# Attention and two expert layers on one core: seven buffers of queries, keys and values, loads six tiles ahead, and their blanks shared out anew

## The chip, the cores and the metric

The kernel runs on one core of a Trainium2 chip. The metric is the device time of one execution in microseconds; less is better. The core has five engines that work side by side: TensorE (PE) multiplies matrices, VectorE (DVE) and ScalarE (ACT) work on elements, GpSimd (POOL) does the same and issues transfers by index, and SyncE (SP) issues most of the ordinary transfers (DMA). Each engine runs its own instructions in program order and waits where data from another is missing.

## The reference

Three layers follow each other. Only the first bears on this change; the other two are expert layers over its result.

```python
q, k, v: (8, 8, 576, 64)              # batch, heads, sequence, head size; float32
scores = scale * matmul(q_c, k_c^T)   # inside chunks of 64 tokens
attn = exp(scores - max) / (sum + 1e-9)
x = matmul(attn, v_c)                 # as (4608, 512): one row for each token
# first expert layer: the best of 8 experts for each token, relu(x @ w1) @ w2, scaled by gates
# second expert layer: 8 experts that take 576 tokens each, in order of their scores
```

## The kernel before

The 4608 tokens are 36 tiles of 128. Attention is one loop over t = 0 to 35 in `attention`. For a tile, `load_qkv` asks SP for two transfers into one of `NQ` buffers named `qkv`, in turn (`t % NQ`): L392 fills the even partitions of columns 0 to 1543 and L393 the odd partitions of columns 1032 to 2575. What the two leave free must be zero, since the products of two heads are made together: `blanks` writes these zeros once for each buffer with two memsets, L379 for the right part (columns 1544 on, before the odd partitions are filled) and L380 for the left part (columns 0 to 1031).

In iteration t the parts stand in this order on every engine: the exponentials of tile t+1 (ACT), the transposes of tile t (`probs_T`, L424), the scores of tile t+2 (`scores`, L403 on PE, maximum L407 and its negative L410 on DVE), the product with the values of tile t-1 (`values`, L439 on PE; L441, L443 and L449 on DVE make and scale the row x), `gates` (L482), the next load (`load_qkv`), the store of x of tile t-1 (`x_out`, L452, also on SP), and the transposes and gate products of older tiles (L459, L470). The order is the program's: PE, DVE, ACT and SP are scheduled by hand.

The load in iteration t is that of tile t+4. With five buffers it overwrites the one of tile t-1, so SP holds it until `values(t - 1)`, a few instructions ahead in the same iteration, is done. The scores of that tile come in iteration t+2.

After every four tiles a routing step (`route`, L499 to L583 on DVE, some rows in each iteration) finds places for 512 tokens, and POOL scatters them into a list with four transfers by index (L585). From t = 23 on the weights of the first expert are fetched (L691), and POOL splits them in two parts (L359, L360). When the loop has ended, job 0 of the first expert layer starts on PE (L824, L844), and the memory of the buffers goes to its weights and its hidden layer.

Of the kernel before, what the change touches and what calls it, by code (L numbers as in the profile page):

```python
# [30 lines left out]
NT = N // 128  # L31
# [21 lines left out]
ROW = 514  # L53
VW = 65
QKV = 2 * 512 + 8 * VW
NQ = 5
T0, T1, T2 = 23, 24, 28
A0, A1, A2, A3 = 5, 2, 1, 1
J0, J1, J2, HOLD2 = 0.8, 0.8, 1, 16
# [9 lines left out]
class Kernel:  # L69
# [226 lines left out]
    def attention(self, st):  # L296
        nc = self.nc
        pool = st.enter_context(self.tc.tile_pool(name="qkvs", bufs=1))
        self.aw = st.enter_context(self.tc.tile_pool(name="aw", bufs=2))
        self.qkvb = []  # L300
        for i in range(NQ):
            a = pool.tile([128, QB], F32, name=f"qkv{i}")
            self.qkvb.append(a)
        for i in range(2):
            self.blanks(i, nc.vector)
            self.load_qkv(i)
        for i in range(2, NQ):
            self.blanks(i, nc.gpsimd)
            if i < 4:
                self.load_qkv(i)  # L310
        spare = self.wk.tile([128, 1], F32, name="spare", bufs=1)
        nc.vector.memset(spare, 0.0)
        nc.scalar.activation(spare, spare, AF.Exp)
        self.constants()
        opened, total, acc = self.opened0, self.total0, self.acc0
        self.state = (acc, opened, total)
        for a, v in ((self.tab, 0.0), (self.order, 0.0), (opened, 0.0), (total, 0.0), (acc, 0.0),
                     (self.L, 0.0), (self.blank, 0.0), (self.left, E * (E - 1) / 2), (self.C, 0.0), (self.first, 0.0), (self.m, -BIG), (self.f, -BIG), (self.dead, -BIG)):
            nc.gpsimd.memset(a, v)
        self.xp = {}  # L320
        self.ex, self.xT, self.x, self.S, self.pending = {}, {}, {}, {}, None
        self.routes, self.scat, self.hold = [], [], 0
        zero = self.qkvb[0][0:128:2, QKV:]
        nc.sync.dma_start(self.list.rearrange("(p r) c -> p (r c)", p=64), zero[:, 0:2 * NB * BT // 64])
        self.scores(0)
        self.scores(1)
        self.exps(0, range(8))
        for t in range(NT):
            if t + 1 < NT:
                self.exps(t + 1, range(4))  # L330
            self.probs_T(t)
            if t + 1 < NT:
                self.exps(t + 1, range(4, 8))
            if t + 2 < NT:
                self.scores(t + 2)
            if t:
                self.values(t - 1)
            self.gates()
            if t + 4 < NT:
                self.load_qkv(t + 4)  # L340
            if t:
                self.x_out(t - 1)
            if t >= 2:
                self.x_T(t - 2)
            if t >= 3:
                self.logits(t - 3)
            self.advance(A0)
            if t == 3:
                self.routes.append(self.select_constants(self.consts))
            if t == T0:  # L350
                self.open(0)
                self.x_list(0)
            c, odd = divmod(t - T0, 2)
            if 0 <= c < 4 and not odd:
                self.fetch(c, self.w1, self.reg)
            c, odd = divmod(t - T1, 2)
            if 0 <= c < 4 and not odd:
                hi, lo = self.chunks[c]
                nc.gpsimd.tensor_copy(hi, self.raw[c])  # L359
                nc.gpsimd.tensor_tensor(lo, self.raw[c], hi.bitcast(F32), op=OP.subtract)  # L360
            if t >= NT - 4:
                self.fetch(t - NT + 4, self.w2, self.reg)
            if t == NT - 1:
                self.x_list(1)
            if t == T2:
                self.x_load(0)
        self.gates()
        self.x_T(NT - 2)
        self.logits(NT - 3)
        for u in (0, 1):  # L370
            self.x_turn(0, u)
        for u in (0, 1):
            self.x_split(0, u)
        self.values(NT - 1)
        self.x_out(NT - 1)

    def blanks(self, i, eng):
        a = self.qkvb[i]
        eng.memset(a[:, QKV:], 0.0)  # L379
        eng.memset(a[:, 0:QKV - 512], 0.0)  # L380

    def finish(self, i):
        self.gates()
# [6 lines left out]
    def load_qkv(self, t):  # L390
        a = self.qkvb[t % NQ]
        self.nc.sync.dma_start(a[0:128:2, 0:QKV], self.qkv[t, 0])  # L392
        self.nc.sync.dma_start(a[1:128:2, QKV - 512:], self.qkv[t, 1])  # L393

    def scores(self, t):
        nc, wk = self.nc, self.aw
        a = self.qkvb[t % NQ]
        q = a[:, QKV - 512:QKV].rearrange("p (h n) -> p h n", h=4)
# [30 lines left out]
    def values(self, t):  # L429
        nc, wk = self.nc, self.aw  # L430
        eT = self.ex.pop(t)
        a = self.qkvb[t % NQ]
        O = [self.ps.tile([128, 4, VW], F32, name="O", bufs=2) for _ in range(2)]
# [989 lines left out]
```

## Time and profile before

| | |
|---|---|
| three runs | 1333.54, 1337.66 and 1338.27 us; median 1337.66 us |
| the profiled execution | 1333.46 us; span from first to last instruction 1331.6 us |
| PE busy in the span | 1157.2 us, 87% |
| attention, 0 to 210 us | PE busy 160.50, DVE 131.00, ACT 107.53, POOL 57.46 us |
| granted PE clock | 0.926 in the mean, 0.87 from 0 to 210 us |
| transfers from 0 to 210 us | 203 GB/s at a busy share of 0.73 |

A time at a row's start counts from the first instruction. The engine of a row that ends in q (SPq) is the queue that issues a transfer: the row's duration is that of the issue, not of the transfer. An arrow in brackets names what ended the idle time before the instruction. The granted clock is a share of 2.4 GHz: 1.00 is that level and 0.50 is 1.2 GHz.

### The profile page before, as it was taken

How to read it: one execution, taken by the hardware profiler on the slowest of the kernel's cores; microseconds unless marked ns; L12 is line 12 of the kernel's file. 1: busy time of each engine (PE TensorE's matmuls, PEld its weight loads, DVE VectorE, ACT ScalarE, POOL GpSimd, SP SyncE). 2: the span in 40 equal slices, each digit the busy share in tenths (PEclk: the TensorE clock that was granted, in tenths of full speed). 3: DMA queues.
4: the chain of work that ended last, by engine and by line, in shares of the span. 5: the costliest groups of instructions: out<-in, count | busy, mean ns of one | idle time of the engine just before them, and what ended most of it. 6: DMA issues, size and time to landing. Idle time of an engine off the chain costs nothing.

```text
span 1331.6 us, 23258 instructions
## 1 busy us (share of the span) xinstructions
PE 1157.2 (87%) x8424; PEld 998.5 (75%) x8424; DVE 776.3 (58%) x2214; ACT 489.6 (37%) x1052; POOL 192.7 (14%) x233
## 2 busy tenths in 40 slices
PE   6978789689898896769789963999999999999997
PEld 4766568688697796768689952878797878788895
DVE  4756687855254354345366667767787868654430
ACT  4655454334242243234244421323232323334430
POOL 3112243111101101110000101020202021112001
PEclk8978789899998897888899975899999999999999
DMA  6776867765353554564467652241515052434310
GB/s 207 235 180 203 202 204 152 198 204 143 109 163 105 151 168 107 161 193 112 123 181 226 206 152 91 76 143 60 168 35 194 14 190 73 138 96 148 114 48 36
DMA packets 90581, 190.06 MB, mean 143 GB/s; under 512 B 22992, under 2 KB 46608, under 8 KB 90384
## 3 DMA queue, kind: packets, MB, share of 16 engines
q1 hardware_dynamic: 77904, 153.96, 39.9%
q0 software_dynamic: 11136, 32.59, 7.7%
q8 instruction: 97, 1.59, 0.6%
q10 hardware_dynamic: 1344, 1.10, 0.3%
q14 instruction: 100, 0.82, 0.2%
HBM read 152.33 MB, written 35.28 MB: 141 GB/s over the span
## 4 chain that ended last, share of the span: by engine, by line
PE 57%; issue 14%; DVE 7%; DMA 5%; POOL 1%; ACT 1%; SPq 1%; ACTq 0%; another core or an unknown queue 0%; POOLq 0%; DVEq 0%
PE O L844 6%; PE ph L844 5%; PE ph L1289 4%; PE ph L1293 4%; PE ph L1291 4%; PE py L1326 3%; PE py L1324 3%; PE py L1328 3%; DMA wr<-in_w_dram 2%; PE O L867 2%; PE O L869 2%; PE O L868 2%; PE ph L867 2%; PE ph L869 2%; PE ph L868 2%
## 5 line engine op out<-in xcount | busy, mean ns | idle before, releaser
L698 DVE TENSOR_TENSOR wlo<-wr,whi 128x1024 fp32r<-128x1024 f32 x122 | 146.6, 1218 | 39.1 <-ACT whi L697 38.4
L1289 PE MATMUL ph<-xhi,whi 128*128 128x256 f32 (+1 forms) x512 | 155.6, 304 | 2.0 <-DVE hlo L1298 0.7
L697 ACT ACTIVATE whi<-wr 128x1024 fp32r<-128x1024 f32 x122 | 126.5, 1054 | 80.8 <-DMA wr<-in_w_dram 37.4
L1291 PE MATMUL ph<-xlo,whi 128*128 128x256 f32 (+1 forms) x512 | 154.7, 302 | 0.0
L1293 PE MATMUL ph<-xhi,wlo 128*128 128x256 f32 (+1 forms) x512 | 154.4, 302 | 0.0
L818 POOL DMA_INDIRECT xr<-xs,idx x48 | 46.3, 965 | 461.9 <-DVE idx L816 143.1
L844 PE MATMUL O<-xhi,whi 128*128 128x256 f32 (+4 forms) x240 | 79.8, 334 | 33.6 <-issue 33.6
L1326 PE MATMUL py<-wlo,hhi 128*128 128x512 f32 x256 | 105.2, 411 | 0.0
L1328 PE MATMUL py<-whi,hlo 128*128 128x512 f32 x256 | 103.0, 402 | 0.0
L1324 PE MATMUL py<-whi,hhi 128*128 128x512 f32 x256 | 102.7, 401 | 0.0
L1297 ACT ACTIVATE hhi<-ph 128x256 fp32r<-128x256 f32 x128 | 49.0, 384 | 145.3 <-PE ph L1293 140.6
L1289 PEld LDWEIGHTS ph<-xhi,whi 128*128 128x128 f32 x512 | 98.5, 192 | 3.9 <-issue 1.1
L1291 PEld LDWEIGHTS ph<-xlo,whi 128*128 128x128 f32 x512 | 98.7, 193 | 0.5 <-DVE xlo L1260 0.2
L1293 PEld LDWEIGHTS ph<-xhi,wlo 128*128 128x128 f32 x512 | 98.5, 192 | 0.4
L844 PE MATMUL ph<-xhi,whi 128*128 128x256 f32 (+4 forms) x240 | 76.8, 324 | 14.1 <-issue 11.4
L1245 DVE TENSOR_TENSOR wlo<-wr,whi 128x512 fp32r<-128x512 f32 x124 | 81.9, 684 | 8.1 <-ACT whi L1240 8.1
L1298 DVE SCALAR_TENSOR_TENSOR hlo<-ph,hhi 128x256 fp32r<-128x256 f32 x128 | 53.0, 419 | 51.5 <-ACT hhi L1297 33.3
L844 PEld LDWEIGHTS O<-xhi,whi 128*128 128x128 f32 x240 | 47.6, 198 | 45.6 <-issue 44.5
L844 PE MATMUL O<-xhi,wlo 128*128 128x256 f32 (+4 forms) x240 | 77.0, 323 | 0.0
L844 PE MATMUL ph<-xhi,wlo 128*128 128x256 f32 (+4 forms) x240 | 74.5, 314 | 0.0
L403 PE MATMUL ph<-qkv 128*64 128x128 f32 x576 | 47.4, 316 | 29.2 <-DMA qkv<-in_qkv_dram 28.5
L417 ACT ACTIVATE ex<-ph,nm 128x64 f32<-128x64 f32 x288 | 68.1, 346 | 11.7 <-DVE nm L410 10.1
(321 smaller groups left out, 2836.8 us busy)
## 6 DMA issues: line engine op xcount, KB each, us to landing
wr<-in_w_dram SPq DMA_DIRECT2D x128, 512.0 KB
qkv<-in_qkv_dram SPq DMA_DIRECT2D x72, 386.0 KB
wr<-in_w2b_dram SPq DMA_DIRECT2D x32, 512.0 KB
wr<-in_w1b_dram SPq DMA_DIRECT2D x30, 512.0 KB
x<-y SPq DMA_DIRECT2D x184, 64.0 KB
xs<-x SPq DMA_DIRECT2D x35, 256.0 KB
x<-blank SPq DMA_DIRECT2D x8, 514.0 KB
wr<-in_w1b_dram ACTq DMA_DIRECT2D x2, 512.0 KB
```

The costliest lines, as they stand in the source:

```text
L417: self.nc.scalar.activation(ex8[:, h // 2, h % 2, :], S8[:, h, :], AF.Exp, scale=0.125, bias=nm[:, h:h + 1])
L697: nc.scalar.activation(hi, self.raw[c], AF.Copy)
L698: (eng or nc.vector).tensor_tensor(lo, self.raw[c], hi.bitcast(F32), op=OP.subtract)
L844: nc.tensor.matmul(p[:, q, :], a[:, k, :], b[:, k, 0:w], start=c == 0, stop=c == 11)
L867: nc.tensor.matmul(q, whi[:, ds], self.hhi[:, f, 0:w], start=f == 0, stop=False)
L1245: self.nc.vector.tensor_tensor(lo[:, s], self.raw[c][:, s], hi[:, s].bitcast(F32), op=OP.subtract)
L1289: nc.tensor.matmul(p, whi[:, k, :], xhi[:, k, cs], start=k == 0, stop=False)
L1291: nc.tensor.matmul(p, whi[:, k, :], xlo[:, k, cs], start=False, stop=False)
L1293: nc.tensor.matmul(p, wlo[:, k, :], xhi[:, k, cs], start=False, stop=k == 3)
L1324: nc.tensor.matmul(p, hhi[:, f, ts], whi, start=f == 0, stop=False)
L1326: nc.tensor.matmul(p, hhi[:, f, ts], wlo, start=False, stop=False)
L1328: nc.tensor.matmul(p, hlo[:, f, ts], whi, start=False, stop=f == 7)
```

## The change

There are seven buffers instead of five. In iteration t the load is that of tile t+6 (`LOOK`), which overwrites the buffer of tile t-1, as before; its scores come in iteration t+4. Ahead of the loop six tiles are loaded instead of four. The zeros are written by other engines: for buffer 0 the left part by DVE and the right one by POOL, for buffer 1 the other way round, and for all others both by POOL; before, DVE wrote both parts of buffers 0 and 1. Buffers 4 to 6 come after the constants.

```diff
-NQ = 5
+NQ = 7
+LOOK = NQ - 1
...
-        for i in range(2):
-            self.blanks(i, nc.vector)
+        self.blanks(0, nc.vector, nc.gpsimd)
+        self.load_qkv(0)
+        self.blanks(1, nc.gpsimd, nc.vector)
+        self.load_qkv(1)
+        for i in (2, 3):
+            self.blanks(i, nc.gpsimd, nc.gpsimd)
             self.load_qkv(i)
-        for i in range(2, NQ):
-            self.blanks(i, nc.gpsimd)
-            if i < 4:
-                self.load_qkv(i)
...
         self.constants()
+        for i in range(4, NQ):
+            self.blanks(i, nc.gpsimd, nc.gpsimd)
+            if i < LOOK:
+                self.load_qkv(i)
...
-            if t + 4 < NT:
-                self.load_qkv(t + 4)
+            if t + LOOK < NT:
+                self.load_qkv(t + LOOK)
...
-    def blanks(self, i, eng):
+    def blanks(self, i, left, right):
         a = self.qkvb[i]
-        eng.memset(a[:, QKV:], 0.0)
-        eng.memset(a[:, 0:QKV - 512], 0.0)
+        right.memset(a[:, QKV:], 0.0)
+        left.memset(a[:, 0:QKV - 512], 0.0)
```

On SP, from the load of tile 3 on, before (the number behind `qkv` is that of the buffer, `list` takes zeros from buffer 0, `xs` takes x of tiles 0 and 1):

```order
L392 DMA qkv3_126<-in_qkv_dram 64x1544
L393 DMA qkv3_126<-in_qkv_dram 64x1544
L324 DMA list_63<-qkv0_123 64x200
L392 DMA qkv4_127<-in_qkv_dram 64x1544
L393 DMA qkv4_127<-in_qkv_dram 64x1544
L392 DMA qkv0_123<-in_qkv_dram 64x1544
L393 DMA qkv0_123<-in_qkv_dram 64x1544
L452 DMA xs_62<-x_308 128x512
L392 DMA qkv1_124<-in_qkv_dram 64x1544
L393 DMA qkv1_124<-in_qkv_dram 64x1544
L452 DMA xs_62<-x_357 128x512
```

And in the changed kernel, where the lines stand five further down:

```order
L397 DMA qkv3_126<-in_qkv_dram 64x1544
L398 DMA qkv3_126<-in_qkv_dram 64x1544
L397 DMA qkv4_127<-in_qkv_dram 64x1544
L398 DMA qkv4_127<-in_qkv_dram 64x1544
L397 DMA qkv5_128<-in_qkv_dram 64x1544
L398 DMA qkv5_128<-in_qkv_dram 64x1544
L329 DMA list_63<-qkv0_123 64x200
L397 DMA qkv6_129<-in_qkv_dram 64x1544
L398 DMA qkv6_129<-in_qkv_dram 64x1544
L397 DMA qkv0_123<-in_qkv_dram 64x1544
L398 DMA qkv0_123<-in_qkv_dram 64x1544
L457 DMA xs_62<-x_318 128x512
```

The store of tile 0's x stood behind the load of tile 5, and now stands behind that of tile 7; the load of tile 5 has moved ahead of the loop.

POOL's start, before (all its six memsets of blanks, then the identity for the transposes):

```order
L379 MEMSET qkv2_125 128x1032
L380 MEMSET qkv2_125 128x1032
L379 MEMSET qkv3_126 128x1032
L380 MEMSET qkv3_126 128x1032
L379 MEMSET qkv4_127 128x1032
L380 MEMSET qkv4_127 128x1032
masks.py:197 MEMSET ident_149 128x128
```

And in the changed kernel:

```order
L384 MEMSET qkv0_123 128x1032
L385 MEMSET qkv1_124 128x1032
L384 MEMSET qkv2_125 128x1032
L385 MEMSET qkv2_125 128x1032
L384 MEMSET qkv3_126 128x1032
L385 MEMSET qkv3_126 128x1032
masks.py:197 MEMSET ident_149 128x128
```

Six memsets still stand ahead of the identity, but the first two are one part each of buffers 0 and 1. The six of buffers 4 to 6 come after the constants, ahead of the zeros for the routing.

## Rows read from the trace of the kernel before

**Rows 1.** The page: engine busy time; the loads of attention.

```profile
PE 1157.2 (87%) x8424; PEld 998.5 (75%) x8424; DVE 776.3 (58%) x2214; ACT 489.6 (37%) x1052; POOL 192.7 (14%) x233
...
qkv<-in_qkv_dram SPq DMA_DIRECT2D x72, 386.0 KB
```

**Rows 2.** Windows: attention as one stretch (columns as in its heading).

```profile
core 0: us, PE busy (x) PEld busy (x) DVE busy (x) ACT busy (x) POOL busy (x), PEclk, DMA share, GB/s
...
0.00:210.00 210.00, 160.50 (x1823) 126.43 (x1824) 131.00 (x552) 107.53 (x386) 57.46 (x96) 0.87 0.73 203
```

**Rows 3.** Waits of PE, 0 to 205 us: total, times, longest.

```profile
PE ph L403 <- DMA qkv<-in_qkv_dram: 28.5, 12, 7.9
...
PE O L439 <- DVE x L449: 5.7, 5, 1.9
```

**Rows 4.** Timeline, first 11 us: start, duration, engine, line, [idle before].

```profile
0.75 0.96 POOL L379 MEMSET qkv<- 128x1032 f32 x1 [0.29 <-POOLq L1411]
...
2.12 0.92 DVE L380 MEMSET qkv<- 128x1032 f32 x1 [0.16 <-issue]
...
3.07 0.59 SPq L392 DMA_DIRECT2D qkv<-in_qkv_dram  x1
...
5.23 0.47 SPq L392 DMA_DIRECT2D qkv<-in_qkv_dram  x1
...
7.86 1.97 PE L403 MATMUL ph<-qkv 128*64 128x128 f32 x16 [7.86 <-DMA qkv<-in_qkv_dram]
...
10.77 1.55 PE L403 MATMUL ph<-qkv 128*64 128x128 f32 x12 [0.94 <-DMA qkv<-in_qkv_dram]
```

**Rows 5.** Timeline: the loads of tiles 5 and 7, and the scores of tile 5.

```profile
18.34 0.47 SPq L392 DMA_DIRECT2D qkv<-in_qkv_dram  x1
...
25.94 1.97 PE L403 MATMUL ph<-qkv 128*64 128x128 f32 x16 [4.12 <-DMA qkv<-in_qkv_dram]
...
29.68 0.47 SPq L392 DMA_DIRECT2D qkv<-in_qkv_dram  x1
```

**Rows 6.** Timeline: scores and values after a wait, and one tile later.

```profile
73.18 1.97 PE L403 MATMUL ph<-qkv 128*64 128x128 f32 x16 [1.88 <-DMA qkv<-in_qkv_dram]
...
74.91 1.98 PE L439 MATMUL O<-qkv,eT 128*64 128x130 f32 x16
...
79.21 1.09 PE L403 MATMUL ph<-qkv 128*64 128x128 f32 x16
...
80.14 1.06 PE L439 MATMUL O<-qkv,eT 128*64 128x130 f32 x16
```

**Rows 7.** Timeline of SP: first half-loads of some tiles.

```profile
20.84 0.47 SPq L392 DMA_DIRECT2D qkv<-in_qkv_dram  x1
...
54.14 0.47 SPq L392 DMA_DIRECT2D qkv<-in_qkv_dram  x1
...
58.03 0.47 SPq L392 DMA_DIRECT2D qkv<-in_qkv_dram  x1
...
64.87 0.47 SPq L392 DMA_DIRECT2D qkv<-in_qkv_dram  x1
...
157.90 0.48 SPq L392 DMA_DIRECT2D qkv<-in_qkv_dram  x1
...
165.63 0.48 SPq L392 DMA_DIRECT2D qkv<-in_qkv_dram  x1
```

**Rows 8.** Windows and timeline around one group's scatters of the list.

```profile
72.00:74.00 2.00, 0.82 (x8) 0.85 (x10) 0.20 (x1) 1.37 (x6) 0.00 (x0) 0.51 1.03 416
...
84.00:88.00 4.00, 2.42 (x32) 2.08 (x28) 0.69 (x1) 1.08 (x5) 1.86 (x2) 1.00 0.91 69
...
87.23 0.69 DVE L407 TENSOR_REDUCE mx<-ph 128x8 f32<-128x512 f32 x1 [4.10 <-remote]
```

**Rows 9.** Timeline: a weight split on POOL and the DVE beside it.

```profile
145.63 2.41 POOL L360 TENSOR_TENSOR wlo<-wr,whi 128x1024 fp32r<-128x1024 f32 x1
...
145.73 2.39 DVE L563 SCALAR_TENSOR_TENSOR ge<-jd,ge 128x72 f32<-128x72 f32 x1
```

## Prediction

> **What bounds it now.** The page says that PE is busy for 87% of the span [rows 1], so only a stretch in which PE stands still can give much. The window of attention shows one: of its first 210 us PE is busy for 160.50, at a granted clock of 0.87, while the DMA engines are busy for 0.73 of the time and move 203 GB/s [rows 2]. No engine is full there: DVE, the next, has 131.00 us. So I read the waits of PE up to 205 us. The scores wait for their loads 12 times, 28.5 us in total; the next group, the values behind DVE's x, has 5.7 us [rows 3]. Two of the twelve are the start, 7.86 and 0.94 us [rows 4]. Ten are left with 19.7 us: the first, 4.12 us ahead of tile 5's scores [rows 5], is the longest, and one of 1.88 us stands at 73.18 [rows 6].
>
> The timeline shows why a load is late. Tile 5's was issued at 18.34, and its scores began at 25.94 when it had landed, 7.6 us later [rows 5]. The load is held until the values of the tile before are done, and its scores come two iterations on. An iteration that neither waits for a load nor holds a scatter takes 3.93 us (mean of 11 distances between SP's loads; 54.14 to 58.03 is one [rows 7]). Two of them are 7.9 us, just what a load took. Whatever delays one stops PE.
>
> A wait costs more than its idle time. Behind the one at 73.18 the scores take 1.97 us and the values 1.98; one tile later 1.09 and 1.06 [rows 6]. The granted clock between 72 and 74 us was 0.51 [rows 8]: PE had stood still and went on at 1.2 GHz. Six of the ten waits have such 1.97 us scores behind them.
>
> **The change, step by step.** *Start.* Tile 0's load went out at 3.07, when DVE had ended its second memset at 3.04. The first ended at 1.96 (2.12 less the 0.16 us idle) and POOL's takes from 0.75 to 1.71 [rows 4]. One part each means that the load can go at about 2.0, 1.1 us earlier. Tile 1's, at 5.23, follows two issues of 0.6 us later, at 3.2. The scores that began at 7.86 and 10.77 each waited for loads, so I take -1.1 us. The bounds are 0, if the constants are next, and -2.0, if the 0.94 us goes too.
>
> *POOL.* It writes 12 blanks instead of six, 6 x 0.96 = 5.8 us more [rows 4]. Ahead of the identity there are six as before, so transposes and constants don't move. The others delay only zeros and constants that the routing reads after several tiles, and POOL is busy for just 57.46 of 210 us [rows 2]. I cost it at nothing; without that cover it would be 5.8 us. On SP the list's zeros now stand behind loads 4 and 5; nobody reads them before the first scatter. Tile 4's blanks come two memsets after the constants, about when its load goes out now.
>
> *Loads six ahead.* Buffers still come free one for each tile, behind the same values, so SP issues as much per iteration as now: nothing is added in the steady state. What changes is how long a load has until its scores: four iterations, about 15.7 us instead of 7.9. The longest wait is 4.12 us, so 7.9 us more hide all ten with room to spare. The ten iterations that hold them take 66.7 us together, the first from 20.84 to 29.68 [rows 5, 7] and the last from 157.90 to 165.63 [rows 7]. At 3.93 us each they would be 39.3. But one of them also holds scatters, and such iterations are long without any wait for a load (58.03 to 64.87 is 6.84 us [rows 7]); I leave it all but its wait, 2.3 us. That makes 66.7 - 39.3 - 2.3 = 25.1 us: the 19.7 us of waits and 5.4 us of slow clock.
>
> *What is late next.* Not all of it can come through. In one of the ten PE also waits 2.3 us for a routing row, and in the last DVE is held about 1.4 us by POOL's split of a weight, as where a row of 0.22 us takes 2.39 beside POOL's 2.41 [rows 9]. Taken off, 21.4 are left. Bounds of this term: 0, if a load asked for earlier lands no earlier; and -31, if beside the 19.7 each of the six slow stretches gives back 1.8 us in scores and values [rows 6].
>
> Job 0 and all that follows hang on the loop by program order, through the last values and the routing; I let its end carry the gain to the end. Sum: -1.1 - 21.4 = -22.5 us. The profiled execution took 1333.46 us, so 1311.0; it is as fast as the fastest run (1333.54), and from the median of 1337.66 the same sum gives 1315.2. Between the two, nearer the median, I say 1314.
>
> **A rule weighed.** In the trace a tile's load took 7.6 us from its issue [rows 5]. The Trainium skill, "DMA: Bandwidth & Descriptors", section "Anatomy of one DMA", gives about 2.0 us and the bytes at 436 GB/s, measured for the path from GpSimd; for two transfers of 386.0 KB an estimate is 3.8 us. By that, two iterations were always enough, the look-ahead was no cause of waiting, and only the start would change, to about 1332.4. The trace disagrees: 7.6 us, and ten waits.
>
> **Rivals.** *The stall moves on* (half the gain). Five of the six long waits follow a group's four scatters. From 84 to 88 us, during one, the DMA engines were 0.91 busy and moved 69 GB/s, and DVE stood still for 4.10 us behind something that the trace can't name [rows 8]. If it is this stall that sets those iterations, and the late load only its last sign, then DVE or the stores are late instead. Left are the start, the wait of 4.12 us with 0.9 of slow clock, and four short waits of 3.3: 9.4 us, so 1324 from the profile and 1328 from the median. For it: the stalls stay. Against it: these iterations are longer still than the scatters' own.
>
> *The transfers are the bound* (no change). If the engines serve late whatever is asked, earlier requests only stand longer in the queue and the waits come back: start alone, 1332.4 to 1336.6. For it: 0.91 busy at 69 GB/s [rows 8]. Against it: 203 GB/s over 210 us is 42.6 MB, which at the 416 GB/s between 72 and 74 us [rows 8] takes 102 us; even with some 4 us for each of seven groups of scatters that is far from 187. The rule of the Trainium skill weighed above ends here too, by another road.
>
> *Crowding* (slower). If up to two more tiles stand in the queues when a scatter comes, each at 772 KB and 416 GB/s 1.9 us, every stall grows by 3.8 us; for seven groups that is 26.6 us, so 4.1 net: 1337.6, and 1341.8 from the median. It decides from 3.2 us per group on. Against it: one load goes out for each buffer freed, as now; only a queue that is already late could hold more.
>
> **How the numbers follow.** Forecast 0.60, half the gain 0.26, transfers 0.08, crowding 0.06. The likeliest's own range is 1305 to 1321. The range has to hold that and the half gain: up to 1330, and down to 1301, where the upper bounds lie (1333.46 - 31 - 2 = 1300.5). A difference under 0.5% (6.7 us) can hardly be told from no change here. Faster by more: 0.60 and nearly all of 0.26, 0.84. Within: 0.11. Slower: 0.05.
>
> **What would show it.** Tile 0's load at about 2.0, and first scores near 6.8. No wait of PE's scores for loads after the start, or one under 1 us. The end of attention's values, near 210 us now, some 22 us earlier. Fewer stretches at 0.50 before it, none behind scores; those behind DVE's routing late in the loop stay. The iterations with scatters still near 6.9 us: if they grow, or if DVE's waits grow by what PE's lose, a rival is right. I am wrong if the loads still arrive late, or if job 0 waits for what the loop no longer hides.

## The result: 1.4% and 0.9% faster, in two measurements

The first measurement gave a median of 1315.86 us (4 runs, 1314.36 to 1318.6) against 1335.6 us for the kernel before in the same session: a ratio of 0.9861, 95% interval 0.982 to 0.9903. In a later session (the run c_after below) it was 1324.24 against 1335.3 us, 0.9908 (0.9874 to 0.9943). The ratios, here and below, are the measurement's own and not quotients of the two medians, which would be 0.9852 and 0.9917. The forecast was 1314 us. The profiled execution took 1314.36 us, 19.1 less than the profiled one of before; its span is 1312.6 us.

The page after, PE's row, which answers to [rows 1]; then the two windows, of which the first answers to [rows 2] and the second ends where attention's loop now ends (busy time of PE, PEld, DVE, ACT and POOL, granted clock, DMA share, GB/s).

```profile
PE 1145.6 (87%) x8424; PEld 988.9 (75%) x8424; DVE 780.9 (59%) x2212; ACT 489.4 (37%) x1052; POOL 197.5 (15%) x239
```

```profile
0.00:210.00 210.00, 172.20 (x2040) 139.47 (x2041) 156.83 (x605) 120.13 (x406) 70.12 (x110) 0.95 0.73 221
...
0.00:187.00 187.00, 149.20 (x1835) 117.22 (x1836) 137.02 (x557) 107.04 (x386) 62.66 (x103) 0.95 0.75 229
```

Set beside [rows 2], the second row is the account of the loop. The same work, to within 12 matmuls, ends 23 us sooner: PE is busy for 149.20 instead of 160.50 us (11.3 less), and stands still for 37.8 instead of 49.5 (11.7 less). The granted clock rose from 0.87 to 0.95: as shares of the two levels that is an estimate of 55 us at 1.2 GHz before (0.13 x 210 x 2) and 19 after (0.05 x 187 x 2). DVE is busy for six us more, though it has two fills less to write.

The later session repeats this only in part. There the rows of c_before and c_after, with the same 1820 matmuls, are

```profile
0.00:207.00 207.00, 158.81 (x1820) 124.67 (x1822) 131.72 (x553) 107.69 (x386) 57.57 (x96) 0.89 0.74 206
```

```profile
0.00:189.50 189.50, 153.03 (x1820) 120.19 (x1822) 136.12 (x551) 107.77 (x386) 62.73 (x102) 0.92 0.74 224
```

PE stands still for 11.7 us less again, but is busy for only 5.8 us less.

PE's waits from 0 to 190 us after (us in total, times, longest), which answer to [rows 3]:

```profile
PE O L444 <- DVE x L454: 13.8, 9, 5.6
PE ph L408 <- DMA qkv<-in_qkv_dram: 6.8, 1, 6.8
PE tp L429 <- ACT ex L422: 5.7, 1, 5.7
PE tp L524 <- DVE roh L518: 3.9, 3, 2.8
```

Of the twelve waits for loads one is left, the first of all. Two others have taken part of their room: the values wait 8.1 us more for DVE's x, and there is a wait of 5.7 us that was not among the waits of before, for ACT's exponentials. The timeline of the start shows where that one comes from (rows of the kernel after, to be read beside [rows 4]):

```profile
1.98 0.59 SPq L397 DMA_DIRECT2D qkv<-in_qkv_dram  x1
...
6.80 1.98 PE L408 MATMUL ph<-qkv 128*64 128x128 f32 x16 [6.80 <-DMA qkv<-in_qkv_dram]
...
8.37 0.95 POOL L384 MEMSET qkv<- 128x1032 f32 x1
...
9.54 7.00 DVE L415 TENSOR_SCALAR nm<-mx 128x8 f32<-128x8 f32 x1
...
11.64 4.91 DVE L412 TENSOR_REDUCE mx<-ph 128x8 f32<-128x512 f32 x1
...
16.30 0.13 POOL L324 MEMSET dead<- 128x50 f32 x1
16.38 0.14 POOL L124 IOTA i<- 128x16 int32 x1
...
16.61 0.17 DVE L415 TENSOR_SCALAR nm<-mx 128x8 f32<-128x8 f32 x1
16.65 2.57 ACT L422 ACTIVATE ex<-ph,nm 128x64 f32<-128x64 f32 x12 [13.35 <-DVE mx L412]
17.31 1.61 PE L429 MATMUL tp<-ident,ex 128*128 128x128 f32 x4 [5.71 <-ACT ex L422]
...
23.80 0.47 SPq L397 DMA_DIRECT2D qkv<-in_qkv_dram  x1
```

The first load and the first scores stand where they were forecast. But DVE's nm, an instruction on 128x8 numbers, takes 7.00 us, where the next one, at 16.61, takes 0.17. Before, the first took 0.55, and the first transposes stood at 12.68:

```profile
10.60 0.55 DVE L410 TENSOR_SCALAR nm<-mx 128x8 f32<-128x8 f32 x1
...
10.98 0.14 POOL L123 IOTA i<- 128x16 int32 x1
...
12.68 1.12 PE L424 MATMUL tp<-ident,ex 128*128 128x128 f32 x4
...
208.85 1.11 PE L439 MATMUL O<-qkv,eT 128*64 128x130 f32 x16
```

It ends at 16.54, just after POOL has come to the end of an unbroken run of fills (buffers 4 to 6 from 8.37 on, then the routing's zeros) and has done an iota (an instruction that writes counting numbers) at 16.38. The kernel before already had the same thing in small: there nm ended at 11.15, just behind the iota at 10.98 that follows the routing's zeros. ACT's exponentials and PE's transposes wait behind nm, so the first load that has to wait for a used buffer (tile 7's, tile 5's before) stands at 23.80 instead of 18.34 [rows 5]. In spite of those 5.5 us the last values, at 208.85 before, are early after:

```profile
184.26 1.70 PE L444 MATMUL O<-qkv,eT 128*64 128x130 f32 x16
```

From the load at 18.34 to the last values it was 190.5 us, and now from 23.80 it is 160.5: the loop itself gained 30.0 us, the start lost 5.5, and 24.6 are left at its end. In the later session the last values moved by 17.6 us (205.62 to 188.03).

### The profile page after: what moved, and what is told of

Same layout as the page of the kernel before. It is cut to its first block, busy times and chain, and to the rows that moved or that the text cites. A ratio compares the mean times of both kernels' runs of the same rounds, so it can differ in the third digit from the quotient of the medians.

```text
span 1312.6 us, 23265 instructions
## 1 busy us (share of the span) xinstructions
PE 1145.6 (87%) x8424; PEld 988.9 (75%) x8424; DVE 780.9 (59%) x2212; ACT 489.4 (37%) x1052; POOL 197.5 (15%) x239
## 4 chain that ended last, share of the span: by engine, by line
PE 52%; issue 14%; DVE 8%; DMA 7%; POOL 2%; ACT 2%; another core or an unknown queue 1%; SPq 0%; POOLq 0%; DVEq 0%; ACTq 0%
PE O L849 5%; PE ph L849 5%; PE ph L1294 4%; PE ph L1296 4%; PE ph L1298 4%; PE py L1331 3%; DMA wr<-in_w_dram 3%; PE py L1329 3%; PE py L1333 3%; DVE wlo L703 2%; PE ph L872 2%; PE s L1011 2%; PE O L872 2%; PE ph L873 2%; PE O L873 2%
## 5 line engine op out<-in xcount | busy, mean ns | idle before, releaser
L849 PEld LDWEIGHTS O<-xhi,whi 128*128 128x128 f32 x240 | 47.6, 198 | 45.4 <-issue 44.2
L849 PE MATMUL O<-xlo,whi 128*128 128x256 f32 (+4 forms) x240 | 70.6, 316 | 0.0
```

The costliest lines, as they stand in the source:

```text
L849: nc.tensor.matmul(p[:, q, :], a[:, k, :], b[:, k, 0:w], start=c == 0, stop=c == 11)
```

## Experiments

**The shares alone: e1_shares_only.** The new shares of the blanks with the old five buffers and loads four ahead.

```diff
-NQ = 7
-LOOK = NQ - 1
+NQ = 5
+LOOK = 4
```

> Five buffers and four tiles ahead as before; only who writes the blanks is as in the changed kernel. My theory (the gain is the loads' look-ahead, and POOL's blanks hold DVE at the start): tile 0's load goes at 2.0 us and its scores start near 6.8, but DVE's first scaling row (L415 there, 0.55 us before) lies beside POOL's memsets from 8.4 us on, now two of 0.95 and thirteen small ones, until about 12.9, so it takes some 3 us and the first exponentials come 1 to 2 us later than before. The waits of the scores for loads stay near 20 us after the start. Time: the same as before, within -2 to +4 us. Rival (the shares bring a part of the gain): 3 us or more faster than before.

Measured: ratio 1.0008 (0.9976 to 1.0041). Behind the start the scores wait for loads 12 times, 17.5 us in all (19.7 before), so the earlier start alone takes next to nothing away. Already here nm is held, for 3.26 us, and the first transposes come at 13.73: fewer fills on POOL, a shorter hold.

**Buffers without look-ahead: e2_look_four.** The changed kernel with loads four ahead.

```diff
-LOOK = NQ - 1
+LOOK = 4
```

> Seven buffers and the changed kernel's blanks, but loads four tiles ahead as before. The load is no longer held by the values of the tile before, only by its place on SP behind the store of an older x. My theory: that alone lets a load go about 2 us earlier; the ten waits of 19.7 us shrink to 4 to 9 us, the start costs the same 5.5 us as in the changed kernel; 1319 to 1328 us. Rival (only the depth counts, an early issue within the iteration is nothing): waits near 19 us, and with the slower start 1336 to 1342 us.

Measured: 0.9956 (0.9925 to 0.9988). PE's waits for loads in this run:

```profile
PE ph L408 <- DMA qkv<-in_qkv_dram: 18.8, 12, 5.8
```

All of them are behind the start. The waits are what the rival expected, about 19 us, and not the 4 to 9 of the theory; the time is better than the rival's by 0.4%. So a load that waits for no buffer is still late if it is asked for only four tiles ahead: only a longer distance between request and use takes the waits away.

**One tile more: e3_six_buffers.** The changed kernel with six buffers, loads five ahead.

```diff
-NQ = 7
+NQ = 6
```

> Six buffers, five tiles ahead. My theory: one iteration more (3.9 us) hides all waits but the longest of 4.12, and one pair of blanks less stands on POOL beside DVE's first scaling row, which takes some 5 us instead of 7.0: 1312 to 1317 us, no wait for loads over 1 us. Rival (depth is needed because transfers as a whole are late): waits halve only, 1321 to 1328 us.

Measured: 0.9858 (0.9803 to 0.9914), on the same chip as e1 and e2. The waits for loads are all but gone, 1.9 us in three, and nm is held for 5.25 us, between e1's and the changed kernel's. One iteration more is enough; the second bought nothing that these runs show.

The windows of e1, e2 and e3 up to the same matmul say that this is not the whole gain (columns as above):

```profile
0.00:212.00 212.00, 163.28 (x1823) 128.81 (x1823) 132.30 (x551) 107.98 (x386) 59.53 (x99) 0.88 0.70 202
```

```profile
0.00:202.00 202.00, 155.78 (x1823) 122.14 (x1823) 135.41 (x550) 107.87 (x386) 62.84 (x102) 0.92 0.78 210
```

```profile
0.00:191.00 191.00, 153.93 (x1823) 120.33 (x1823) 134.19 (x551) 107.49 (x386) 60.94 (x101) 0.92 0.76 224
```

From e1 to e2, with two more buffers at the same distance, PE is busy for 7.5 us less at a higher clock, although its waits for loads didn't shrink; from e2 to e3, with the longer distance, it stands still for 9.2 us less, 1.8 of them at the start. From the first transposes to the last values e1 takes 196.7 us (13.73 to 210.39), e2 183.6 (17.33 to 200.89) and e3 173.5 (15.51 to 189.04). So in these three profiles about half of the loop's gain comes with the free buffers alone. By what road is not shown; in the medians, 1342.97, 1336.84 and 1321.21 us, it is the smaller part.

**The blanks off POOL: e4_blanks_on_act.** The blanks of buffers 4 to 6 are copied by ACT from a zero (`zb`, set by DVE ahead of what is shown), so POOL's run of fills at the start is six shorter; the constants come behind them.

```diff
...
-        self.constants()
         for i in range(4, NQ):
-            self.blanks(i, nc.gpsimd, nc.gpsimd)
+            a = self.qkvb[i]
+            for part in (a[:, QKV:], a[:, 0:QKV - 512]):
+                nc.scalar.activation(part, zb.to_broadcast([128, QKV - 512]), AF.Copy)
...
+        self.constants()
```

> The changed kernel with the blanks of buffers 4 to 6 copied from a zero by ACT, which is idle then, instead of POOL's memsets. My theory (POOL's run of memsets holds DVE's first scaling row for 7.0 us, and the loop starts 5 us late by it): that row takes 1 to 2 us, the first transposes start near 12.5 us instead of 17.3, and attention ends 4 to 5 us earlier: 1309 to 1313 us. Rival (what is late at the start is made good in the loop, whose end is set by the routing on DVE): the start moves, the end doesn't, 1314 to 1318 us.

Measured: 0.983 (0.9787 to 0.9873). nm takes 0.84 us and the first transposes stand at 11.93. But the changed kernel's trace was from another session, and beside it this run's lead of 5.4 us in the values up to 57 us had turned into 2.3 us of lag at the last values (186.60 against 184.26). So the two were run again side by side, with the kernel before for its trace.

**On one chip: c_before, c_after, e4_again.** Unchanged copies of the three.

> The kernel before once more, for its profile on the same chip as the three that follow. Both theories: the end of the attention's loop at about 210 us and the span within 0.5% of 1335.

> The changed kernel once more, on the same chip as the kernel before and the two that follow. Theory (what is given back in the expert layers is chance from run to run): the attention's loop ends 22 to 26 us earlier than in the kernel before on this chip, and the later layers keep it to within 3 us or lose up to 5 at random. Rival (the change itself makes the expert layers slower): the same loss of 4 to 5 us at the same place, between 500 and 640 us. Ratio 0.982 to 0.990 either way.

> The blanks of buffers 4 to 6 on ACT, now on the same chip as the changed kernel. Theory (the run of POOL's fills holds VectorE at the start and costs 5 us, which the loop then keeps): scores of tile 1 some 5 us earlier than in the changed kernel, and the time 3 to 5 us shorter than the changed kernel's. Rival (the late loop is limited by something else, so the early 5 us are lost before its end): 5 us earlier up to 62 us, level with the changed kernel at the loop's end to within 2 us, and the time within 2 us of the changed kernel's.

Measured: 1337.7 us for the one run of c_before, whose last values stand at 205.62; 0.9908 (0.9874 to 0.9943) for c_after and 0.9852 (0.9809 to 0.9895) for e4_again, medians of 1324.24 and 1316.42 us. The start of c_after, then of e4_again:

```profile
9.05 7.52 DVE L415 TENSOR_SCALAR nm<-mx 128x8 f32<-128x8 f32 x1
...
17.34 0.79 PE L429 MATMUL tp<-ident,ex 128*128 128x128 f32 x2 [6.43 <-ACT ex L422]
...
188.03 2.00 PE L444 MATMUL O<-qkv,eT 128*64 128x130 f32 x16
```

```profile
10.07 1.09 DVE L419 TENSOR_SCALAR nm<-mx 128x8 f32<-128x8 f32 x1
...
11.93 1.47 PE L433 MATMUL tp<-ident,ex 128*128 128x128 f32 x4 [1.14 <-ACT ex L426]
...
183.51 2.00 PE L448 MATMUL O<-qkv,eT 128*64 128x130 f32 x16
```

The transposes are 5.4 us earlier and the last values 4.5: in this pair the loop keeps the start, which is against the rival (a late loop that swallows it). The medians differ by 7.8 us, more than the theory's 3 to 5. The price of the hold stays rough: the last values of one kernel differ by 3 to 4 us between sessions (184.26 and 188.03, 186.60 and 183.51), so a single pair of profiles hardly fixes 4.5, and it is the two ratios for each kernel (0.983 and 0.9852 against 0.9861 and 0.9908) that agree on the direction. c_after's 17.6 us at the loop's end lies below both theories' 22. Its loss in the expert layers came where the rival said: matmul by matmul it is 16.0 us ahead of c_before at 482 us and 10.5 at 638. I come back to that below.

**POOL's splits off POOL as well: e5_no_pool_split.** As e4, and ACT and DVE do the splits of the first expert's weights that POOL did late in the loop. The splits also come three iterations later (T1).

```diff
-T0, T1, T2 = 23, 24, 28
+T0, T1, T2 = 23, 27, 28
...
-                hi, lo = self.chunks[c]
-                nc.gpsimd.tensor_copy(hi, self.raw[c])
-                nc.gpsimd.tensor_tensor(lo, self.raw[c], hi.bitcast(F32), op=OP.subtract)
+                self.split(0, c)
```

> As the last, and the splits of the first expert's weights that POOL did late in the loop are done by ACT and VectorE instead. Theory (VectorE's short instructions, held for 1.6 to 3.2 us behind POOL's splits, are what TensorE waits for in the late loop): the waits of the values' matmuls for VectorE's x fall from about 12 us in all to below 5, the loop ends 3 to 6 us earlier than in the last run, and the time is 2 to 6 us shorter. Rival (VectorE's own share, 4 splits of about 1.2 us, costs as much as the holds): the waits for x stay at 8 to 14 us and the time within 2 us of the last run's.

Measured: 0.9834 (0.9793 to 0.9875), 1315.17 us, 1.25 under e4_again. Their waits for DVE's x, e4_again's first:

```profile
PE O L448 <- DVE x L458: 13.6, 9, 5.2
```

```profile
PE O L446 <- DVE x L456: 5.6, 7, 1.8
```

The holds were real and the waits fall, from 13.6 to 5.6 us, but the time moves by less than the 2 us of the rival, and the last values come 0.6 us earlier (182.87 against 183.51) instead of 3 to 6. The splits now take DVE 1.22 us each. The theory's mechanism held and its gain didn't; that the one pays for the other is argued, not shown.

**What ends a hold: f1_iota_between.** The changed kernel with an iota of one column on POOL behind the two fills of each of buffers 4 to 6.

```diff
             self.blanks(i, nc.gpsimd, nc.gpsimd)
+            nc.gpsimd.iota(gap[:, i - 4:i - 3], pattern=[[0, 1]], base=0, channel_multiplier=1,
+                           allow_small_or_imprecise_dtypes=True)
```

> The changed kernel, with one iota of a single column on POOL behind the two fills of each of buffers 4, 5 and 6. Theory (VectorE's held instruction gets in when POOL's unbroken run of fills ends, and an iota ends it): the iota behind buffer 4's fills stands at about 10.2 us, VectorE's nm that takes 7.00 us in the changed kernel ends there and takes about 1 us, TensorE's first transposes stand at 12 to 13 us instead of 17.3, and the time is 2 to 6 us under the changed kernel's (ratio to before 0.982 to 0.987). Rival (the hold lasts until all of POOL's fills are done, whatever stands between): nm still takes about 7 us, the first transposes stand at 17 us and the ratio is the changed kernel's, 0.986 to 0.991.

Measured: 0.9801 (0.9774 to 0.9828), 1292.31 us on a chip where the kernel before took 1317.46. The start:

```profile
10.18 0.12 POOL L319 IOTA gap<- 128x1 f32 x1
...
10.77 1.35 DVE L418 TENSOR_SCALAR nm<-mx 128x8 f32<-128x8 f32 x1
...
12.06 0.12 POOL L319 IOTA gap<- 128x1 f32 x1
...
12.69 1.31 DVE L418 TENSOR_SCALAR nm<-mx 128x8 f32<-128x8 f32 x1
12.89 1.61 PE L432 MATMUL tp<-ident,ex 128*128 128x128 f32 x4 [0.96 <-ACT ex L425]
...
13.94 0.12 POOL L319 IOTA gap<- 128x1 f32 x1
```

Both nm end with an iota, at 12.12 and 14.00 us, the third iota ending at 14.06; the fills go on to 16.7 behind them. The first iota, at 10.18, was over before nm began. So the hold lasts as long as fill follows fill without a break, and one instruction of 0.12 us ends it. The other profiles agree: in each, the first nm ends within 0.06 us of the end of one of POOL's iotas. The transposes stand at 12.89, as expected, and the ratio is better than expected. It is the best of all that ran; whether it beats e4 is open, since they ran on different chips and their intervals overlap.

The absolute time can't be set beside the others. The last values of f1 are 14 to 18 us earlier than the changed kernel's elsewhere:

```profile
169.82 1.11 PE L447 MATMUL O<-qkv,eT 128*64 128x130 f32 x16
```

Only about 4.4 us of that come from the start; most of the rest comes in the iterations with scatters, and on this chip the kernel before is 18 to 23 us faster than on the others as well. No trace of the kernel before or of the changed kernel was taken there.

**Scatters twice: f2_before_twice, f3_after_twice.** Each list scatter of the loop is issued a second time, into a list that nobody reads.

```diff
+            self.disjoint(self.scat2, nc.gpsimd.indirect_dma_start(
+                out=self.list2[:, :], out_offset=bass.IndirectOffsetOnAxis(ap=idx[:, i:i + 1], axis=0),
+                in_=xm[:, i, :], in_offset=None))
```

> The kernel before with each list scatter of the attention's loop issued twice (the second into a list that nobody reads). Theory (the scatters hold up the transfers, and that is what makes the loads late): the scores' waits for loads rise from 28 us in all to 40 or more, and the loop's end moves from about 207 us to 225 to 245. Rival (the loads are late by their number and buffers alone): waits for loads stay at 24 to 32 us, and the loop's end moves by less than 8 us, by what POOL issues more.

> The changed kernel with each list scatter issued twice in the same way. Theory (the look-ahead absorbs what a scatter delays): waits for loads stay below 10 us in all, the start's 6.8 among them, and the loop's end moves by at most half of what it moves in the kernel before with doubled scatters. Rival (a doubled scatter stops the engines themselves, not only the loads): the loop's end moves as far as in the kernel before with doubled scatters, with waits on VectorE and POOL in place of loads.

Measured: 1.0232 (1.0194 to 1.027) for the kernel before so changed, 1.01 (1.0069 to 1.0131) for the changed one. Their waits for loads, f2's first:

```profile
PE ph L405 <- DMA qkv<-in_qkv_dram: 47.6, 18, 7.8
```

```profile
PE ph L410 <- DMA qkv<-in_qkv_dram: 18.6, 5, 9.2
```

In the kernel before the waits rise from 28.5 [rows 3] to 47.6 us, as the theory had it, so scatters do make loads late. How far the loop's end moves can't be read against traces from other chips, as f1 showed: the last values stand at 216.47 in f2 and 195.31 in f3, the latter 25.5 us behind f1, which has the iotas too. The times on this chip say more. f2 takes 33.7 us more than the kernel before (1351.12 against 1317.46); f3, at 1330.0, takes 25 to 31 us more than the changed kernel would by its two ratios (an estimate of 1299 to 1305). So a doubled scatter costs the changed kernel most of what it costs the kernel before, which is on the rival's side, and f3's total of 18.6 misses the 10 that I allowed. Nearly all that is new there is one wait, of 9.22 us, and around it the trace shows a stop of everything but POOL, in the windows (columns as above) and in the timeline:

```profile
136.00:140.00 4.00, 0.00 (x0) 0.00 (x0) 0.00 (x0) 0.00 (x0) 3.08 (x4) 0.87 0.80 235
140.00:144.00 4.00, 0.00 (x0) 0.00 (x0) 0.00 (x0) 0.00 (x0) 3.08 (x4) 0.50 1.13 260
```

```profile
116.23 0.69 SPq L400 DMA_DIRECT2D qkv<-in_qkv_dram  x1
134.79 0.51 SPq L399 DMA_DIRECT2D qkv<-in_qkv_dram  x1
...
144.62 1.97 PE L410 MATMUL ph<-qkv 128*64 128x128 f32 x16 [9.22 <-DMA qkv<-in_qkv_dram]
...
145.87 0.75 DVE L456 TENSOR_TENSOR x<-O,rs 128x256 f32<-128x256 f32 x2 [12.45 <-DMA xs<-x]
```

SP issues no load for 18 us, and DVE waits 12.45 us for a store of x. What SP waits for is no buffer. Ahead of the next load in its order stands the read of the list for job 0 (L819 in f3), and that waits for the scatters to be done (SP's waits from 110 to 150 us, then the timeline):

```profile
SPq L819 <- DMA list<-xm,idx: 14.3, 1, 14.3
```

```profile
133.71 0.42 SPq L819 DMA_DIRECT2D meta<-list  x1
```

In the changed kernel the same wait (L814) is 3.0 us. Loads and stores stand behind it because SP issues in order, and a request six tiles ahead doesn't help while its issuer stands still. That scatters by themselves stop PE, f3 doesn't show: during the first group's eight PE is busy all the time.

```profile
56.00:66.00 10.00, 10.00 (x144) 8.17 (x144) 8.08 (x39) 8.02 (x29) 7.67 (x8) 1.00 0.88 156
```

## Why the prediction was right

The sum came out in the first session, 19.1 us between the profiled executions where 22.5 was forecast, and partly by luck: the loop gained 30.0 us instead of 21.4, and against that stand 5.5 us lost at the start, where 1.1 was to be gained, and another 5.5 lost behind the loop. In the later session the medians differ by 11.1 us, half of the sum.

*Start, -1.1 us: right for the load and the scores.* The load went out at 1.98 and the first scores began at 6.80. What that is worth on its own no run shows: in e1 the hold of nm already turns it into transposes 1.05 us later than in the first profile of before.

*POOL, "I cost it at nothing": wrong.* This is the term that failed. I looked for who reads what the six fills delay, and nobody does. I didn't ask what a run of fills does to DVE beside it, although the record had DVE held beside POOL's split [rows 9]. It put the loop's first load into a used buffer 5.5 us later; e4_again had 4.5 us of it back at the loop's end in one pair on one chip, by taking just these fills off POOL. That it is the unbroken run that holds DVE, f1 shows.

*Loads six ahead, 25.1 us: the mechanism right as far as it goes, the size somewhat small.* All ten waits behind the start are gone, as forecast (one of 0.6 us is left in c_after), and e2 and e3 show that the distance of the request does it: with four ahead 18.8 us of waits are left, with five 1.9. But the prediction put the whole gain down to those waits, and e2 shows a part that comes with the free buffers while the waits stay. The loop gained 30.0 us in the first session and 24.4 in the second (from the loads at 17.86 and 24.62 to the last values), where 25.1 less 3.7 was forecast. The slow clock was put at 5.4 us: PE's busy time fell by 11.3 in the first pair, near the upper bound of six slow stretches at 1.8 us each, and by 5.8 in the second, which is the size forecast. I had counted the time lost up to SP's next load; in the first pair the slow rows reach further, with an estimate of 55 us at 1.2 GHz before and 19 after.

*What is late next, 3.7 us: too small.* The values' waits for DVE's x alone grew by 8.1 us. DVE is now the late one, held again by POOL in the weight splits; in e5, where the splits went to ACT and DVE, those waits shrank and no time was gained.

*The end carries the gain: in good part.* In the first pair 24.6 us at the loop's end became 19.1 at the end of the profiled runs, in the second 17.6 became 11.0. Most of the loss sits in the expert layers. Matmul by matmul against c_before, seven of ten profiles with the new shares (e1 among them, which has nothing else new) lose 3.8 to 5.4 us between 482 and 638 us and f3 2.6, while e2 and e4_again lose less than 1. The first profile of before loses 0.5 there, f2 1.3. Nothing in those layers was changed, and one kernel shows both: e4 loses 4.0 in its first profile and 0.1 in its second. Why most runs with the new shares lose it stays open; no experiment was aimed at it.

*Rivals.* "The stall moves on" was half right: the long iterations stay. An undisturbed iteration is 3.44 us between loads in the changed kernel (39.77 to 43.21), the first with scatters still 6.85 (55.06 to 61.91), as forecast. But how long depends on more than the kernel: on the chip of f1 the first four scatters fall into iterations of 3.49 and 4.34 us. "The transfers are the bound" fell: the same bytes went at 229 GB/s instead of 203. "Crowding" did not show at the given number of scatters: the first group's iteration didn't grow, and the time fell.

The loads of the changed kernel, from which the last numbers are:

```profile
39.77 0.47 SPq L397 DMA_DIRECT2D qkv<-in_qkv_dram  x1
43.21 0.47 SPq L397 DMA_DIRECT2D qkv<-in_qkv_dram  x1
...
55.06 0.47 SPq L397 DMA_DIRECT2D qkv<-in_qkv_dram  x1
61.91 0.47 SPq L397 DMA_DIRECT2D qkv<-in_qkv_dram  x1
```

## What to carry to other kernels

A prefetch hides its waits by the distance between its request and its use: compare the time from issue to use with the iterations between them, and stop one iteration past that. Then see what stands in front of the load on the engine that issues it, since a request can't be early behind an instruction that waits. Count with a PE wait the slow matmuls behind it too; here they were worth 6 to 11 us beside 11.7 us of standing still. Work moved onto an idle POOL isn't free if DVE has short instructions on the critical path meanwhile: break its run of fills, or give them to ACT.

## What the runs showed of the hardware

DVE's nm (a tensor_scalar on 128x8 float32) took 7.00 and 7.52 us beside POOL's run of fills, 5.25, 3.26 and 0.84 with shorter runs, about 1.3 where an iota of 0.12 us broke the run, and 0.17 with no fill beside it; no single fill took more than 0.96. Whether a pause, or another instruction than an iota, ends the hold as well was not tried. The instruction behind it, mx, took 4.91 us instead of 0.69, from inside nm's time to just behind its end.

The Trainium skill, "SBUF — State Buffer", section "Who interferes with whom", has the ground of this: a tensor_scalar can run in a mode that takes the port pair which DVE shares with GpSimd, and then whoever issues first holds the pair for the whole instruction while the other is blocked. The traces agree that it is nm that is blocked, but the hold lasted over a whole run of fills, not over one. That nm ran in such a mode no trace shows.
